# Loading keys, values and the output weights over two DMA queues in a decode kernel

## The chip, the cores and the metric

The kernel runs on one core of a Trainium2 chip. The metric is the device time of one execution in microseconds (us). Every kernel below was run several times, in turn with the kernel before on the same chip. The profiled executions give a span that is some 2 us shorter than the time (136.1 us of span go with 138.0 us). In the profiles, PE is TensorE, DVE is VectorE, ACT is ScalarE and SP is SyncE; the small q (SPq) marks an instruction that issues a load. A ring is the list of loads that one engine has issued and that are not yet done; I use the word for the queue of one issuing engine. The granted clock is the share of its full clock that TensorE ran at.

## The reference

One token of a decoder layer: attention over the last 4096 cached positions of 16 key/value heads, beside a two-layer GELU block, mixed by a sigmoid gate. Cut to what matters:

```python
# D = 576, Hq = 32, Hkv = 16, Dh = 128, window W = 4096, F = 4608, all bf16
q = (x @ wq)                                   # wq: 4.7 MB
scores = q . k[last 4096] / sqrt(128)          # k: 16 heads x 1 MB
o = softmax(scores) . v[last 4096]             # v: 16 heads x 1 MB
a = o @ wo                                     # wo: 4.7 MB
b = gelu(x @ w1 + b1) @ w2 + b2                # w1, w2: 5.3 MB each
g = sigmoid(sum(x * gate_w))
return g * a + (1 - g) * b
```

Every weight and every cached key and value is used once. The work is to move 53.6 MB from HBM, the chip's main memory, into the core.

## The kernel before

All large loads are issued from SyncE, on one queue, in the order w1, wq, K, V, wo, w2. K and V tiles of 1 MB share a pool of 8 buffers. The parts that matter here:

```python
    kv_pool = ctx.enter_context(tc.tile_pool(name="kv_pool", bufs=8, side="right"))
    ...
    for h in range(Hkv):                              # scores
        k_t = kv_pool.tile([P, NCH * Dh], BF16, name="kv_t", tag="kv")
        nc.sync.dma_start(out=k_t[:], in_=A_k_cache[0, h, Sk - W : Sk, :]...)
        kt = early[:, (h % 2) * W : (h % 2 + 1) * W]
        nc.vector.transpose(out=kt.bitcast(FP32), in_=k_t[:].bitcast(FP32))
        ...                                           # 8 matmuls into s_ps
    ...                                               # softmax -> pt
    for h in range(Hkv):                              # values
        v_t = kv_pool.tile([P, NCH, Dh], BF16, name="kv_t", tag="kv")
        nc.sync.dma_start(out=v_t[:], in_=A_v_cache[0, h, Sk - W : Sk, :]...)
        for c in range(NCH):
            nc.tensor.matmul(o_ps[:, 2 * h : 2 * h + 2], lhsT=v_t[:, c, :], ...)
    ...
    for r in range(0, RO, 8):                         # wo: 4 chunks, 1152 KB each
        nc.sync.dma_start(out=wo_t[:, r : r + 8, :], in_=wo_src[:, r : r + 8, :])
    cuts = [(0, 0, 9), (0, 9, 18), (1, 0, 8), (1, 8, 13), (1, 13, 16), (1, 16, 18)]
    for b, j0, j1 in cuts:                            # w2: 6 chunks
        nc.sync.dma_start(out=w2_t[:, b * NJ + j0 : b * NJ + j1, :], in_=...)
    ...                                               # o_ps -> o_sb -> om -> ov
    for r in range(RO):                               # 32 pairs of products
        y_add(ov[:, r : r + 1], wo_t[:, r, :])
    for f in range(NF):                               # 36 pairs of products
        y_add(gt[:, f : f + 1], w2_t[:, f, :], stop=(f == NF - 1))
```

`y_add` makes one pair of matmuls with a single output row: 512 columns and 64 columns. I call it a pair. wo_t takes the space of wq_t, and w2_t that of w1_t, so both can load as soon as q and the hidden layer are computed. That is long before they are needed. The source order of the loads is not binding: the framework has a scheduler that orders the instructions of each engine itself, and it may move a load forward.

Of the kernel before, what the change touches and what calls it, by code (L numbers as in the profile page):

```python
# [9 lines left out]
BF16 = mybir.dt.bfloat16  # L10
# [6 lines left out]
def kernel(  # L17
# [15 lines left out]
    nc = tc.nc  # L33

    P = 128
    D = 576
    Hq, Hkv, Dh = 32, 16, 128
    Sk, W = 32768, 4096
    NCH = W // P
# [13 lines left out]
    kv_pool = ctx.enter_context(tc.tile_pool(name="kv_pool", bufs=8, side="right"))  # L53
# [72 lines left out]
    for t in range(2):  # L126
# [18 lines left out]
        out=junk_row[:],  # L145
# [17 lines left out]
        out=omg[:], in0=g_t[:], scalar1=-1.0, scalar2=1.0, op0=ALU.mult, op1=ALU.add  # L163
# [3 lines left out]
        out=b2g[:], in0=b2_row[:], scalar1=omg[0:1, 0:1], scalar2=None, op0=ALU.mult  # L167
# [38 lines left out]
    for j in range(NJ):  # L206
# [15 lines left out]
        out=poly[:],  # L222
# [50 lines left out]
    for b in range(4):  # L273
# [4 lines left out]
            out=diag[:, :, 0:512].rearrange("p h (j m) -> p h j m", m=P)[:, :, :, 0:2],  # L278
            in_=qj_ps[rows].rearrange("p j h t -> p h j t"),
# [3 lines left out]
    s_ps = ps_s.tile([P, NCH * 32], FP32, name="s_ps")  # L283
    for h in range(Hkv):
        k_t = kv_pool.tile([P, NCH * Dh], BF16, name="kv_t", tag="kv")
        nc.sync.dma_start(
            out=k_t[:],
            in_=A_k_cache[0, h, Sk - W : Sk, :].rearrange("(p c) d -> p (c d)", p=P),
        )
        kt = early[:, (h % 2) * W : (h % 2 + 1) * W]  # L290
        nc.vector.transpose(out=kt.bitcast(FP32), in_=k_t[:].bitcast(FP32))  # L291
        kv = kt.rearrange("p (c b k t) -> p c b k t", c=NCH, b=2, t=2)
        for j in range(4):
            for f in range(2):
                nc.tensor.matmul(  # L295
                    s_ps[:, f * 512 : (f + 1) * 512].rearrange("p (c k) -> p c k", k=32),
                    lhsT=qz[:, h, j, :],
                    rhs=kv[:, f * 16 : (f + 1) * 16, j // 2, :, j % 2],
                    start=(h == 0 and j == 0),
                    stop=(h == Hkv - 1 and j == 3),  # L300
                    skip_group_check=True,
                )


    m1 = const.tile([P, 1], FP32, name="m1")
# [6 lines left out]
    for b in range(4):  # L312
# [10 lines left out]
        out=e_t[:], in_=s_ps[:], func=ACT.Exp, bias=negm[:, 0:1], scale=SCALE, accum_out=sums[:]  # L323
# [13 lines left out]

    o_ps = ps_o.tile([P, Hq], FP32, name="o_ps")
    for h in range(Hkv):
        v_t = kv_pool.tile([P, NCH, Dh], BF16, name="kv_t", tag="kv")  # L340
        nc.sync.dma_start(
            out=v_t[:],
            in_=A_v_cache[0, h, Sk - W : Sk, :].rearrange("(p c) d -> p c d", p=P),
        )
        for c in range(NCH):
            nc.tensor.matmul(  # L346
                o_ps[:, 2 * h : 2 * h + 2],
                lhsT=v_t[:, c, :],
                rhs=pt[:, c, 2 * h : 2 * h + 2],
                start=(c == 0),  # L350
                stop=(c == NCH - 1),
            )
# [3 lines left out]
    wo_t = big.tile([P, RO, D], BF16, name="wo_t", tag="A")  # L356
    wo_src = A_wo.rearrange("(p r) n -> p r n", r=RO)
    for r in range(0, RO, 8):
        nc.sync.dma_start(out=wo_t[:, r : r + 8, :], in_=wo_src[:, r : r + 8, :])
    w2_t = big.tile([P, NF, D], BF16, name="w2_t", tag="B")  # L360
    w2_src = B_w2.rearrange("(b p j) n -> p b j n", b=2, j=NJ)
    cuts = [(0, 0, 9), (0, 9, 18), (1, 0, 8), (1, 8, 13), (1, 13, 16), (1, 16, 18)]
    for b, j0, j1 in cuts:
        nc.sync.dma_start(
            out=w2_t[:, b * NJ + j0 : b * NJ + j1, :], in_=w2_src[:, b, j0:j1, :]
# [6 lines left out]
    for a in range(4):  # L372
        nc.vector.tensor_scalar(
            out=om[:, :, a], in0=o_sb[:], scalar1=hi4[:, a : a + 1], scalar2=None, op0=ALU.mult
# [47 lines left out]
```

## Time and profile before

| | before |
|---|---|
| time, median | 138.0 us (137.85 to 138.01) |
| span | 136.1 us |
| bytes loaded | 53.8 MB |
| DMA rate, plateau | about 420 GB/s |
| last V product starts | 108.4 us |
| first wo product starts | 111.2 us |
| last y product ends | 133.1 us |

First, part 2 of the page of the kernel before: the span in 40 slices of 3.4 us, one digit per slice. PE and DMA are busy tenths, PEclk is the granted clock of TensorE in tenths, and GB/s is what the DMA engines moved.

```profile
PE   0099999352997978768774239453352459987891
...
PEclk9999999999999999999999655555555555799999
DMA  4999999999999999999999999999999999999940
GB/s 122 423 425 421 420 419 419 408 420 412 421 421 424 419 417 421 419 417 424 419 421 414 419 421 424 412 421 412 417 421 414 427 427 406 433 417 426 403 182 0
```

The DMA row is full from the second slice until the thirty-eighth, and the rate is flat. At 420 GB/s, 53.8 MB take 128 us. The kernel is bound by its loads from one end to the other. The page's list of DMA queues names their packets, bytes and share of the engines' time. Queue q1 belongs to SyncE and q10 to ScalarE:

```profile
q1 hardware_dynamic: 7490, 53.61, 95.6%
...
q10 hardware_dynamic: 8, 0.01, 0.0%
```

One queue alone keeps the engines occupied for 95.6% of the span. The chain of work that ended last (part 4 of the page), by engine and by line, says the same:

```profile
## 4 chain that ended last, share of the span: by engine, by line
DMA 77%; DVE 9%; PE 9%; issue 2%; SPq 1%; ACT 0%; DVEq 0%
DMA kv_t<-in_A_v_cache_dram 27%; DMA kv_t<-in_A_k_cache_dram 27%; DMA w_t<-in_B_w_dram 24%; DVE early L291 9%; PE s_ps L295 5%; PE y_ps L174 3%; PE o_ps L346 1%; SPq L76 1%; PE y_ps L177 0%; DVE out_row L390 0%; ACT out_row L389 0%; DVEq L291 0%
```

These are lines of PE's timeline before: start and duration in us, line, tiles and shapes, how many instructions were merged, and in brackets the idle time before them and what ended it.

```profile
80.34 5.26 PE L346 MATMUL o_ps<-pt,kv_t 128*128 128x2 bf16 x192 [2.59 <-DVE pt L335]
...
108.37 1.01 PE L346 MATMUL o_ps<-pt,kv_t 128*128 128x2 bf16 x32 [1.48 <-DMA kv_t<-in_A_v_cache_dram]
110.41 0.21 PE L377 MATMUL ov_ps<-lo32b,om 128*128 128x32 bf16 x1 [1.02 <-DVE om L373]
111.17 0.59 PE L174 MATMUL y_ps<-wo_t,ov 128*1 128x512 bf16 x1 [0.55 <-DMA wo_t<-in_A_wo_dram]
...
122.71 0.38 PE L174 MATMUL y_ps<-w_t,gt 128*1 128x512 bf16 x1 [0.63 <-DMA w_t<-in_B_w_dram]
...
132.75 0.38 PE L174 MATMUL y_ps<-w_t,gt 128*1 128x512 bf16 x1
```

The softmax lets the V products start at 80.34. V15, the last V tile, is consumed from 108.37, o is rearranged into ov, and the first wo product starts at 111.17. The 68 pairs end at 133.1, and here and there they wait for w2 (0.63 us in the fifth line). A pair takes 0.48 us while the granted clock is 0.50, and 0.245 us at 1.00. There were 12 slow pairs here. So about 12 x 0.48 + 56 x 0.245 = 19.5 us of products after V are hidden under the 24 us in which wo and w2 load (10.0 MB at 420 GB/s). The issue times on SyncE's queue show that order (start, time from first to last issue, line, tiles, count):

```profile
53.33 36.63 SPq L341 DMA_DIRECT2D kv_t<-in_A_v_cache_dram  x16
90.89 7.82 SPq L359 DMA_DIRECT2D wo_t<-in_A_wo_dram  x4
100.86 13.39 SPq L364 DMA_DIRECT2D w_t<-in_B_w_dram  x6
```

### The profile page before, as it was taken

Reading aid. Unit: us, or ns where it says so; the run is one execution under the profiler, and the core shown is the slowest. Engines: PE = TensorE matmul, PEld = TensorE weight load, DVE = VectorE, ACT = ScalarE, POOL = GpSimd, SP = SyncE. Lnnn points to the kernel's source line nnn. Section 1 sums busy time; section 2 is a strip of 40 time slices with the busy share of each in tenths; the row PEclk is TensorE's granted clock in tenths of the full one; section 3 lists DMA queues with packets and bytes.
Section 4 is the critical chain, followed back from the end, with each engine's and each line's share of the span. In section 5 each row is a group of like instructions: output and inputs, shape, how many; then the busy total and the mean of one; then the engine's idle time right before and its main releaser. Section 6 shows DMA issues by size and latency. Waiting matters only on the chain.

```text
span 136.1 us, 2522 instructions
## 1 busy us (share of the span) xinstructions
PE 90.0 (66%) x1140; PEld 54.9 (40%) x1140; DVE 53.4 (39%) x83; ACT 3.8 (3%) x8; POOL 0.7 (1%) x6
## 2 busy tenths in 40 slices
PE   0099999352997978768774239453352459987891
PEld 0089599341342323323231239452342433433340
DVE  5873002228689999989974250000000030000001
ACT  3000000000000000000000300000000000000001
POOL 2000000000000000000000000000000000000000
PEclk9999999999999999999999655555555555799999
DMA  4999999999999999999999999999999999999940
GB/s 122 423 425 421 420 419 419 408 420 412 421 421 424 419 417 421 419 417 424 419 421 414 419 421 424 412 421 412 417 421 414 427 427 406 433 417 426 403 182 0
DMA packets 7509, 53.79 MB, mean 395 GB/s; under 512 B 837, under 2 KB 841, under 8 KB 1481
## 3 DMA queue, kind: packets, MB, share of 16 engines
q1 hardware_dynamic: 7490, 53.61, 95.6%
q8 instruction: 9, 0.15, 0.4%
q14 instruction: 2, 0.02, 0.0%
q10 hardware_dynamic: 8, 0.01, 0.0%
HBM read 53.62 MB, written 0.00 MB: 394 GB/s over the span
## 4 chain that ended last, share of the span: by engine, by line
DMA 77%; DVE 9%; PE 9%; issue 2%; SPq 1%; ACT 0%; DVEq 0%
DMA kv_t<-in_A_v_cache_dram 27%; DMA kv_t<-in_A_k_cache_dram 27%; DMA w_t<-in_B_w_dram 24%; DVE early L291 9%; PE s_ps L295 5%; PE y_ps L174 3%; PE o_ps L346 1%; SPq L76 1%; PE y_ps L177 0%; DVE out_row L390 0%; ACT out_row L389 0%; DVEq L291 0%
## 5 line engine op out<-in xcount | busy, mean ns | idle before, releaser
L295 PE MATMUL s_ps<-early 128*128 128x512 bf16 x128 | 32.6, 401 | 10.5 <-DVE early L291 10.5
L291 DVE STREAM_TRANSPOSE early<-kv_t 128x2048 f32<-128x2048 f32 x16 | 36.6, 2304 | 3.6 <-DMA kv_t<-in_A_k_cache_dram 1.9
L346 PE MATMUL o_ps<-pt,kv_t 128*128 128x2 bf16 x512 | 15.4, 165 | 16.2 <-DMA kv_t<-in_A_v_cache_dram 13.7
L295 PEld LDWEIGHTS <-early 128*128 128x128 bf16 x128 | 12.8, 100 | 29.9 <-issue 16.3
L346 PEld LDWEIGHTS <-kv_t 128*128 128x128 bf16 x512 | 14.8, 105 | 17.1 <-DMA kv_t<-in_A_v_cache_dram 14.5
L370 DVE COPY o_sb<-o_ps 128x32 f32<-128x32 f32 x1 | 0.2, 191 | 29.1 <-PE o_ps L346 29.1
L174 PE MATMUL y_ps<-wo_t,ov 128*1 128x512 bf16 x32 | 10.9, 471 | 0.6 <-DMA wo_t<-in_A_wo_dram 0.6
L174 PE MATMUL y_ps<-w_t,gt 128*1 128x512 bf16 x36 | 9.2, 379 | 1.8 <-DMA w_t<-in_B_w_dram 1.8
L390 DVE CAST out_row<-y_ps 1x320 bf16<-1x320 f32 x1 | 0.5, 478 | 22.8 <-ACT out_row L389 22.8
L198 PE MATMUL h_ps<-xt,w_t 128*128 128x1 bf16 x144 | 9.3, 201 | 0.0
L198 PEld LDWEIGHTS <-w_t 128*128 128x128 bf16 x144 | 9.1, 167 | 0.2 <-issue 0.2
L177 PE MATMUL y_ps<-wo_t,ov 128*1 128x64 bf16 x32 | 7.0, 218 | 0.0
L177 PE MATMUL y_ps<-w_t,gt 128*1 128x64 bf16 x36 | 6.9, 192 | 0.0
L174 PEld LDWEIGHTS <-ov 128*1 128x1 bf16 x32 | 3.2, 100 | 6.6 <-issue 3.8
L245 PE MATMUL q_ps<-xt,wq_t 128*128 128x1 bf16 x128 | 3.9, 165 | 2.3 <-DMA wq_t<-in_A_wq_dram 2.3
L174 PEld LDWEIGHTS <-gt 128*1 128x1 bf16 x36 | 3.0, 84 | 4.8
L245 PEld LDWEIGHTS <-wq_t 128*128 128x128 bf16 x128 | 3.7, 105 | 2.4 <-DMA wq_t<-in_A_wq_dram 2.4
L216 DVE COPY hacc<-h_ps 128x36 f32<-128x36 f32 x1 | 0.2, 195 | 11.1 <-PE h_ps L207 11.1
L177 PEld LDWEIGHTS <-gt 128*1 128x1 bf16 x36 | 3.0, 84 | 2.1 <-issue 2.1
L140 DVE MEMSET early<- 128x4160 f32 x1 | 3.5, 3525 | 0.8 <-issue 0.8
L177 PEld LDWEIGHTS <-ov 128*1 128x1 bf16 x32 | 3.0, 94 | 0.2 <-issue 0.2
L187 PE MATMUL h_ps<-one_b,b_row 1*128 1x1 bf16 x36 | 2.4, 196 | 0.3 <-DMA b_row<-in_B_b_dram 0.3
(75 smaller groups left out, 31.5 us busy)
## 6 DMA issues: line engine op xcount, KB each, us to landing
kv_t<-in_A_k_cache_dram SPq DMA_DIRECT2D x16, 1024.0 KB, 18.2
kv_t<-in_A_v_cache_dram SPq DMA_DIRECT2D x16, 1024.0 KB, 17.5
w_t<-in_B_w_dram SPq DMA_DIRECT2D x5, 1152.0 KB, 9.0
wo_t<-in_A_wo_dram SPq DMA_DIRECT2D x4, 1152.0 KB, 20.5
wq_t<-in_A_wq_dram SPq DMA_DIRECT2D x4, 1024.0 KB, 13.6
w_t<-in_B_w_dram SPq DMA_DIRECT2D x2, 1296.0 KB
w_t<-in_B_w_dram SPq DMA_DIRECT2D x1, 720.0 KB, 22.0
w_t<-in_B_w_dram SPq DMA_DIRECT2D x1, 576.0 KB
```

The source lines that it names most:

```text
L76: nc.sync.dma_start(out=w1_m[:, k, :], in_=w1_src[:, k, :])
L140: nc.vector.memset(qz_flat.bitcast(FP32), 0.0)
L174: nc.tensor.matmul(y_ps[0:1, 0:N0], lhsT=vec, rhs=row[:, 0:N0], start=start, stop=stop, skip_group_check=True)
L177: nc.tensor.matmul(y_ps[0:1, N0:D], lhsT=vec, rhs=row[:, N0:D], start=start, stop=stop, skip_group_check=True)
L187: nc.tensor.matmul(h_ps[:, c : c + 1], lhsT=b1_row[0:1, f0 : (c // NJ + 1) * FH : NJ], rhs=one_b[0:1, 0:1], start=(c == 0), stop=False, sk ...
L198: nc.tensor.matmul(h_ps[:, c : c + 1], lhsT=w1_m[:, k, f0 : (c // NJ + 1) * FH : NJ], rhs=xt[:, k : k + 1], start=False, stop=False, skip_ ...
L216: nc.vector.tensor_copy(out=hacc[:], in_=h_ps[:])
L245: nc.tensor.matmul(q_ps[:, j : j + 1], lhsT=wq_m[:, k, j * Dh : (j + 1) * Dh], rhs=xt[:, k : k + 1], start=(k == 0 and j == 0), stop=False ...
L291: nc.vector.transpose(out=kt.bitcast(FP32), in_=k_t[:].bitcast(FP32))
L295: nc.tensor.matmul(s_ps[:, f * 512 : (f + 1) * 512].rearrange("p (c k) -> p c k", k=32), lhsT=qz[:, h, j, :], rhs=kv[:, f * 16 : (f + 1) * ...
L346: nc.tensor.matmul(o_ps[:, 2 * h : 2 * h + 2], lhsT=v_t[:, c, :], rhs=pt[:, c, 2 * h : 2 * h + 2], start=(c == 0), stop=(c == NCH - 1),)
L390: nc.vector.tensor_copy(out=out_row[:, 0:320], in_=y_ps[0:1, 0:320])
```

## The change

The intent: odd K and V tiles and every other wo chunk are issued from ScalarE instead of SyncE, so that the DMA engines are fed by two rings. The first eight V loads also move up in the source, ahead of the softmax, so that ScalarE issues its part of them before its exponential. In full:

```diff
--- before.py
+++ after.py
@@ -283,7 +283,7 @@
     s_ps = ps_s.tile([P, NCH * 32], FP32, name="s_ps")
     for h in range(Hkv):
         k_t = kv_pool.tile([P, NCH * Dh], BF16, name="kv_t", tag="kv")
-        nc.sync.dma_start(
+        (nc.sync if h % 2 == 0 else nc.scalar).dma_start(
             out=k_t[:],
             in_=A_k_cache[0, h, Sk - W : Sk, :].rearrange("(p c) d -> p (c d)", p=P),
         )
@@ -301,6 +301,16 @@
                     skip_group_check=True,
                 )
 
+    def load_v(h):
+        v_t = kv_pool.tile([P, NCH, Dh], BF16, name="kv_t", tag="kv")
+        (nc.sync if h % 2 == 0 else nc.scalar).dma_start(
+            out=v_t[:],
+            in_=A_v_cache[0, h, Sk - W : Sk, :].rearrange("(p c) d -> p c d", p=P),
+        )
+        return v_t
+
+    v_tiles = [load_v(h) for h in range(8)]
+
 
     m1 = const.tile([P, 1], FP32, name="m1")
     nc.vector.reduce_max(out=m1[:], in_=s_ps[:], axis=AX.X)
@@ -337,11 +347,7 @@
 
     o_ps = ps_o.tile([P, Hq], FP32, name="o_ps")
     for h in range(Hkv):
-        v_t = kv_pool.tile([P, NCH, Dh], BF16, name="kv_t", tag="kv")
-        nc.sync.dma_start(
-            out=v_t[:],
-            in_=A_v_cache[0, h, Sk - W : Sk, :].rearrange("(p c) d -> p c d", p=P),
-        )
+        v_t = v_tiles[h] if h < 8 else load_v(h)
         for c in range(NCH):
             nc.tensor.matmul(
                 o_ps[:, 2 * h : 2 * h + 2],
@@ -356,7 +362,9 @@
     wo_t = big.tile([P, RO, D], BF16, name="wo_t", tag="A")
     wo_src = A_wo.rearrange("(p r) n -> p r n", r=RO)
     for r in range(0, RO, 8):
-        nc.sync.dma_start(out=wo_t[:, r : r + 8, :], in_=wo_src[:, r : r + 8, :])
+        (nc.sync if r % 16 == 0 else nc.scalar).dma_start(
+            out=wo_t[:, r : r + 8, :], in_=wo_src[:, r : r + 8, :]
+        )
     w2_t = big.tile([P, NF, D], BF16, name="w2_t", tag="B")
     w2_src = B_w2.rearrange("(b p j) n -> p b j n", b=2, j=NJ)
     cuts = [(0, 0, 9), (0, 9, 18), (1, 0, 8), (1, 8, 13), (1, 13, 16), (1, 16, 18)]
```

## The prediction

> **What bounds the kernel now.** The loads. The page's 40 slices show all 16 DMA engines at 9 tenths or more from the second slice to the thirty-eighth and about 420 GB/s. 53.8 MB at that rate is 128 us of the 136.1 us span. The chain of waits agrees: DMA 77%. The last large w2 chunk releases PE at 128.6, PE runs to 133.2, the output takes until 136.1.
>
> This works because of the order of loads: V before wo before w2. The last V tile's matmuls start at 108.4 (PE's timeline); o is finished and the first wo product starts at 111.2; then 68 pairs of y products follow, 0.48 us a pair for the first 5.7 us (granted clock 0.50) and 0.245 us after (clock 1.00). These 19.6 us hide under the 24 us in which wo and w2 load.
>
> **What the change adds and moves.** No bytes and no PE or DVE instructions. Half of K, V and wo is issued from ScalarE.
>
> 1. Rate. The intent is more bandwidth from two rings. The engines show no gaps. The Trainium skill, "DMA: Bandwidth & Descriptors", section "Issuing engines are not separate DMA queues", says that all issuers' DMAs interleave on the same 16 engines and only issue time is saved; an issue here takes 0.33 us against 2.5 us for the megabyte it moves. I expect the plateau to stay at 415 to 430 GB/s.
>
> 2. Order. In the built instruction order of the changed kernel, the first two wo chunks come before the last K tiles, the last two between V1 and V4, and the first two w2 chunks before V8 to V15 on the SyncE queue. So 7.4 MB (17.5 us) that used to come after V now comes ahead of its second half. After V14 on that ring there is only 2.65 MB of w2, 6.3 us.
>
> 3. Late start of odd K tiles: ScalarE issues K1 only after its exponential at 23.3, and K3 to K7 around the q copies at 30. SyncE has four queued by then. Tiles land in pairs: the first transpose about 2 us later.
>
> **Costed, as estimates from these durations.** The total load still ends near 131. wo ahead of K (5.6 us) and pairing (about 2 us) move scores and softmax from 80 to about 88. The last V tile now lands 6.3 us before the loads end, with landing time near 126 instead of 108. Then: two V heads 2.0, o to ov 1.8, 68 pairs 19.6 (the same 5.7 us at half clock), output 2.9. Sum: 152 us span, plus the 1.9 us between span and time.
>
> **Prediction: 153.5 us**, range 147 to 159. Faster by over 2%: 0.03; within 2%: 0.04; slower: 0.93.
>
> **What would show each step.** Right: the second hardware queue carries about 20 MB; GB/s flat near 420 until about 128 us, then near zero; the chain of waits ends in V load, V products, then over 18 us of y products; the first wo product starts near 130; PE never waits for w2. Wrong on step 1: a plateau above 432. Wrong on step 2: wo products starting before 120, or waits for w2 between them.
>
> **What would make it wrong.** Two rings lifting the rate by several per cent; rings not shared evenly, which could bring V14 earlier; gaps in DMA where queue slots and buffers wait for one another; the clock staying low through all 68 pairs (up to 13 us more).

## The result and the profile after

The changed kernel takes 152.79 us (median of 4 runs, 152.51 to 153.61) against 137.95 us. The ratio is 1.109, with a 95% interval from 1.104 to 1.113. Ratios here are the mean time of one kernel's runs over the mean of the other's runs of the same rounds, so they are not quite the ratio of the medians.

Part 2 of the page after (slices of 3.8 us):

```profile
PE   0299996225968776872097117441104445699992
...
PEclk9999999999999999999569965555555555599999
DMA  5999999999999999999999999999999999700000
GB/s 142 424 426 419 418 418 412 421 420 416 422 422 422 416 420 421 417 422 422 418 423 415 423 423 419 422 421 415 422 413 422 420 414 416 292 1 0 4 0 0
```

The rate is the same as before. But the loads end in the thirty-fifth slice, near 130 us. Then the DMA is idle and PE works alone for five slices. The queues share the bytes, and together they occupy the engines for as many microseconds as one queue did: 86.4% of 150.6 us is 130 us, and 95.6% of 136.1 us is 130 us.

```profile
q1 hardware_dynamic: 4898, 34.48, 55.7%
q10 hardware_dynamic: 2600, 19.15, 30.7%
```

In the chain of work after, the y products (L174 and L177) have grown from 3% to 12%:

```profile
## 4 chain that ended last, share of the span: by engine, by line
DMA 76%; PE 14%; DVE 6%; issue 2%; SPq 1%; ACT 0%; DVEq 0%
DMA kv_t<-in_A_v_cache_dram 28%; DMA kv_t<-in_A_k_cache_dram 27%; DMA w_t<-in_B_w_dram 21%; PE y_ps L174 11%; DVE early L291 5%; PE y_ps L177 1%; PE o_ps L352 1%; SPq L76 1%; DVE om L381 0%; DVE out_row L398 0%; ACT out_row L397 0%; PE ov_ps L385 0%; DVE ov L389 0%; DVE o_sb L378 0%; DVEq L291 0%
```

PE's timeline after, from the softmax to the first wo product:

```profile
90.07 2.70 PE L352 MATMUL o_ps<-pt,kv_t 128*128 128x2 bf16 x96 [2.59 <-DVE pt L345]
...
126.00 1.86 PE L352 MATMUL o_ps<-pt,kv_t 128*128 128x2 bf16 x64 [1.40 <-DMA kv_t<-in_A_v_cache_dram]
128.89 0.21 PE L385 MATMUL ov_ps<-lo32b,om 128*128 128x32 bf16 x1 [1.02 <-DVE om L381]
129.38 0.58 PE L174 MATMUL y_ps<-wo_t,ov 128*1 128x512 bf16 x1 [0.28 <-DVE ov L389]
```

and its last product of 512 columns:

```profile
147.27 0.38 PE L174 MATMUL y_ps<-w_t,gt 128*1 128x512 bf16 x1
```

V15 is consumed 18 us later than before, and everything behind it shifts with it. The group of w2 products in the after page shows no idle time before any of its 36 instructions (last number):

```profile
L174 PE MATMUL y_ps<-w_t,gt 128*1 128x512 bf16 x36 | 9.0, 380 | 0.0
```

Before, this group had waited 1.8 us for w2; after, the weights had been there for a long time. SyncE's issues in the trace after show why:

```profile
47.33 0.33 SPq L365 DMA_DIRECT2D wo_t<-in_A_wo_dram  x1
...
65.95 0.33 SPq L365 DMA_DIRECT2D wo_t<-in_A_wo_dram  x1
...
80.95 8.19 SPq L372 DMA_DIRECT2D w_t<-in_B_w_dram  x2
91.09 11.43 SPq L306 DMA_DIRECT2D kv_t<-in_A_v_cache_dram  x4
112.74 5.79 SPq L372 DMA_DIRECT2D w_t<-in_B_w_dram  x4
```

Two wo chunks (one here, one on ScalarE's queue at 47.2) are issued amid K. Two more come amid the first V tiles, and the first two w2 chunks come before V8, V10, V12 and V14. In the kernel before, all of this came after V15.

### The profile page after: what moved, and what is told of

The parts are those of the page before. It is cut to its first block, busy times and chain, and to the rows that moved or that the text cites. A ratio compares the mean times of both kernels' runs of the same rounds, so it can differ in the third digit from the quotient of the medians.

```text
span 150.6 us, 2526 instructions
## 1 busy us (share of the span) xinstructions
PE 88.4 (59%) x1140; PEld 54.1 (36%) x1140; DVE 53.0 (35%) x83; ACT 3.8 (3%) x8; POOL 0.7 (0%) x6
## 3 DMA queue, kind: packets, MB, share of 16 engines
q10 hardware_dynamic: 2600, 19.15, 30.7%
## 4 chain that ended last, share of the span: by engine, by line
DMA 76%; PE 14%; DVE 6%; issue 2%; SPq 1%; ACT 0%; DVEq 0%
DMA kv_t<-in_A_v_cache_dram 28%; DMA kv_t<-in_A_k_cache_dram 27%; DMA w_t<-in_B_w_dram 21%; PE y_ps L174 11%; DVE early L291 5%; PE y_ps L177 1%; PE o_ps L352 1%; SPq L76 1%; DVE om L381 0%; DVE out_row L398 0%; ACT out_row L397 0%; PE ov_ps L385 0%; DVE ov L389 0%; DVE o_sb L378 0%; DVEq L291 0%
## 5 line engine op out<-in xcount | busy, mean ns | idle before, releaser
L295 PE MATMUL s_ps<-early 128*128 128x512 bf16 x128 | 33.6, 410 | 17.1 <-DVE early L291 17.0
L352 PE MATMUL o_ps<-pt,kv_t 128*128 128x2 bf16 x512 | 14.9, 165 | 25.5 <-DMA kv_t<-in_A_v_cache_dram 22.9
L174 PE MATMUL y_ps<-wo_t,ov 128*1 128x512 bf16 x32 | 9.4, 426 | 0.3 <-DVE ov L389 0.3
L174 PE MATMUL y_ps<-w_t,gt 128*1 128x512 bf16 x36 | 9.0, 380 | 0.0
L177 PE MATMUL y_ps<-w_t,gt 128*1 128x64 bf16 x36 | 6.9, 193 | 0.0
L177 PE MATMUL y_ps<-wo_t,ov 128*1 128x64 bf16 x32 | 6.6, 205 | 0.0
L174 PEld LDWEIGHTS <-ov 128*1 128x1 bf16 x32 | 2.9, 92 | 5.6 <-issue 2.0
L174 PEld LDWEIGHTS <-gt 128*1 128x1 bf16 x36 | 3.0, 84 | 4.8
L177 PEld LDWEIGHTS <-gt 128*1 128x1 bf16 x36 | 3.1, 85 | 0.0
L177 PEld LDWEIGHTS <-ov 128*1 128x1 bf16 x32 | 2.9, 89 | 0.0
```

What stands on the lines that cost most here:

```text
L174: nc.tensor.matmul(y_ps[0:1, 0:N0], lhsT=vec, rhs=row[:, 0:N0], start=start, stop=stop, skip_group_check=True)
L177: nc.tensor.matmul(y_ps[0:1, N0:D], lhsT=vec, rhs=row[:, N0:D], start=start, stop=stop, skip_group_check=True)
L295: nc.tensor.matmul(s_ps[:, f * 512 : (f + 1) * 512].rearrange("p (c k) -> p c k", k=32), lhsT=qz[:, h, j, :], rhs=kv[:, f * 16 : (f + 1) * ...
```

## The experiments

Eight kernels were run, all correct. Where an order had to be forced, the loads were chained by scheduling edges, which order the instructions that the scheduler emits and add no wait; so they fix the order on each ring, but do not hold one ring back for the other:

```python
    def in_order(keys):
        for first, then in zip(keys, keys[1:]):
            tc.add_manual_dep(loads[then].ins, loads[first].ins.name,
                              <NoSync edge>, reason="order of loads")
```

Theory A: the order of the loads costs the time, because bytes that V does not need now arrive before V, and the products behind V come out from under the loads. Theory B, the rival: two rings cost the time themselves, through tiles that arrive in pairs, late issue on ScalarE, or contention. Theory C, the intent: two rings raise the rate.

Times are medians. Spans and first wo products are those of the one profiled execution, which can be the fastest of its runs (w2 after V: 149.25 us) or the slowest (wo alone: 141.23, V15 moved: 146.29).

| run | rings | ahead of the last V tile, beyond before | first wo product | span | time | ratio (95%) |
|---|---|---|---|---|---|---|
| before | 1 | - | 111.2 | 136.1 | 138.0 | 1 |
| source move only | 1 | - | 111.3 | 136.2 | 137.99 | 1.000 (0.998 to 1.001) |
| both rings, old order | 2 | - | 113.5 | 137.0 | 138.66 | 1.005 (1.003 to 1.008) |
| wo alone on both | 2 | 2 wo chunks, 2.4 MB | 116.9 | 139.5 | 140.42 | 1.017 (1.015 to 1.019) |
| w2 after V, V15 moved | 2 | wo, 4.7 MB | 122.4 | 144.5 | 146.04 | 1.059 (1.057 to 1.060) |
| w2 after V | 2 | wo, 4.7 MB (w2 beside V15) | 125.9 | 147.5 | 150.02 | 1.087 (1.083 to 1.091) |
| w2 products ahead | 2 | wo and 2 w2 chunks, 7.4 MB | 129.1 | 146.0 | 148.16 | 1.075 (1.071 to 1.078) |
| changed kernel | 2 | wo and 2 w2 chunks, 7.4 MB | 129.4 | 150.6 | 152.79 | 1.109 (1.104 to 1.113) |
| new order on one ring | 1 | the same 7.4 MB | 128.3 | 150.1 | 152.02 | 1.101 (1.099 to 1.104) |
| all of w2 before V8 | 2 | wo and all w2, 10.0 MB | 135.6 | 157.0 | 159.13 | 1.154 (1.149 to 1.159) |

### Both rings, the old order

The changed kernel, with all wo and w2 loads behind V15:

```diff
+    # every wo and w2 load gets a scheduling edge from every V load
+    after_all((nc.sync if r % 16 == 0 else nc.scalar).dma_start(out=wo_t[...], ...))
+    after_all(nc.sync.dma_start(out=w2_t[...], ...))
```

> Both rings exactly as in the changed kernel (odd K, V and half of wo from ScalarE), but the order of loads of the kernel before is forced: all K, all V, then wo, then w2. Theory A (the order of loads costs the time, two rings in themselves are neutral): 137 to 140 us, DMA plateau near 420 GB/s, first wo product near 111 to 113 us, and the chain of waits ends in w2 loads again. Rival B (two rings in themselves cost it, by pairing of tiles, by ScalarE issuing late or by contention): above 145 us although the order is restored. Rival C (two rings raise the rate): below 135 us.

Measured: 138.66 us, 0.5% above the kernel before; the first wo product came at 113.5, a little later than the expected 111 to 113. PE's timeline of this run:

```profile
84.34 6.62 PE L368 MATMUL o_ps<-pt,kv_t 128*128 128x2 bf16 x243 [2.60 <-DVE pt L361]
...
111.00 1.01 PE L368 MATMUL o_ps<-pt,kv_t 128*128 128x2 bf16 x32 [2.23 <-DMA kv_t<-in_A_v_cache_dram]
...
113.52 0.58 PE L190 MATMUL y_ps<-wo_t,ov 128*1 128x512 bf16 x1 [0.28 <-DVE ov L405]
...
129.49 0.38 PE L190 MATMUL y_ps<-w_t,gt 128*1 128x512 bf16 x1 [0.44 <-DMA w_t<-in_B_w_dram]
```

With the order restored, 14.1 of the 14.8 us are gone, and the w2 products wait for w2 again (last line). Theory B keeps 0.7 us at most, and theory C gets nothing: the loads ran near 420 GB/s, as before. The 0.7 us has a visible counterpart. Softmax ends at 84.3 instead of 80.3, and the table of engines by stretch (length, busy time and count of PE, PEld, DVE, ACT, POOL, then clock, DMA share and GB/s) shows the one gap in the loads, in the stretch from 85 to 88 us:

```profile
85.00:88.00 3.00, 3.00 (x119) 3.00 (x116) 0.00 (x0) 0.00 (x0) 0.00 (x0) 0.50 0.90 344
```

The kernel before had a DMA share of 1.01 there. The loss from 85 to 91 us, against 420 GB/s, is (3 x 76 + 3 x 8) / 420 = 0.6 us. That the eight V buffers had run out while the softmax was late fits this, but I did not test it.

### The new order on one ring

The converse: no load from ScalarE, but the merged order of the changed kernel.

```diff
-    (nc.sync if h % 2 == 0 else nc.scalar).dma_start(...)     # K, V, wo
+    nc.sync.dma_start(...)
+    in_order(K0..K12, wo0, wo1, K13..K15, V0..V2, wo2, wo3, V3..V7,
+             w2_0, w2_1, V8..V15, w2_2..w2_5)
```

> The converse: every load from SyncE on one ring, in the merged order of the changed kernel (two wo chunks before K13, two between V2 and V3, two w2 chunks before V8). Theory A: 150 to 154 us, with the last V products near 126 to 127 and y products for over 17 us after all loads have ended. Rival B: near 138 us.

Measured: 152.02 us. Its GB/s row and PE's timeline:

```profile
GB/s 155 423 425 422 412 421 412 420 413 424 419 421 419 415 421 422 427 413 424 419 417 421 424 419 419 416 418 419 419 419 419 421 411 421 329 10 0 4 0 0
```

```profile
125.76 1.01 PE L367 MATMUL o_ps<-pt,kv_t 128*128 128x2 bf16 x32 [1.48 <-DMA kv_t<-in_A_v_cache_dram]
...
128.28 0.58 PE L189 MATMUL y_ps<-wo_t,ov 128*1 128x512 bf16 x1 [0.28 <-DVE ov L413]
```

One ring with the new order reproduces the loss to 0.8 us; the last V products start at 125.8, just before the expected 126 to 127. Together with the run before this settles theory A against B: the order carries the time, and the number of rings hardly matters (0.7 to 0.8 us in these two runs).

### The w2 products moved ahead

The order of loads on each queue is that of the changed kernel. PE does the 18 pairs of the first two w2 chunks where it waits for V8.

```diff
+        if h == 8:
+            for f in range(NJ):
+                y_add(gt[:, f : f + 1], w2_t[:, f, :], behind=o_mm)
...
-    for f in range(NF):
+    for f in range(NJ, NF):
```

A first build without the edge behind V7's products let the scheduler put nine of these matmuls ahead of all V products.

> The changed kernel with its order of loads on each queue unchanged, but PE does the 18 pairs of products of the first two w2 chunks between V7 and V8, where it sits idle for 6.9 us and where both chunks have landed. If the added time is the exposed chain of y products, 18 pairs at 0.245 us leave it: 4.4 us less than the changed kernel, 147.5 to 149.5 us, loads ending at the same time. If instead the late end is set by something else, 152.8 stays.

Measured: 148.16 us, 4.6 us less than the changed kernel. PE's timeline of this run, the first of the 18 pairs and the first wo product:

```profile
105.44 0.59 PE L189 MATMUL y_ps<-w_t,gt 128*1 128x512 bf16 x1
...
129.06 0.58 PE L189 MATMUL y_ps<-wo_t,ov 128*1 128x512 bf16 x1 [0.28 <-DVE ov L424]
```

The loads still end near 130 us and the first wo product comes within 0.3 us of the changed kernel's (129.38), but the last y product starts at 142.6 instead of 147.3. The exposed time at the end is therefore the chain of y products, pair by pair.

### All of w2 after V, with wo still early

```diff
-             w2_0, w2_1, V8..V15, w2_2..w2_5)
+             V8..V15, w2_0..w2_5)
```

> Two rings, wo early as in the changed kernel, but all of w2 after V15. Theory A: two w2 chunks (2.65 MB, 6.3 us at 420 GB/s) no longer stand before the last V tile, so it lands 6.3 us sooner and the whole tail with it: 152.8 - 6.3 = 146.5 us, range 145 to 148.5. PE then does the w2 products without waiting. Rival B: 152 to 153.

Measured: 150.02 us. The direction is that of theory A, but only about half of the 6.3 us came back. The timeline:

```profile
117.72 1.86 PE L367 MATMUL o_ps<-pt,kv_t 128*128 128x2 bf16 x64 [3.28 <-DMA kv_t<-in_A_v_cache_dram]
123.36 1.01 PE L367 MATMUL o_ps<-pt,kv_t 128*128 128x2 bf16 x32 [3.77 <-DMA kv_t<-in_A_v_cache_dram]
...
125.88 0.58 PE L189 MATMUL y_ps<-wo_t,ov 128*1 128x512 bf16 x1 [0.28 <-DVE ov L411]
```

V13 and V14 are done at 117.7 + 1.9, but V15 is used only from 123.4, where a tile takes 2.5 us to arrive elsewhere in this trace (a pair every 5.0). My sum had treated the two rings as one line. V15 was the last load on ScalarE's ring while SyncE's ring had already gone on to w2, so w2 took about half of the rate while V15 loaded. The packet records of this trace show it: from 117 to 121 us SyncE's ring moved 223 GB/s and ScalarE's 188, and from 100 to 115, with V tiles on both, 209 and 208.

### The same with V15 on SyncE's ring

```diff
-        (nc.sync if h % 2 == 0 else nc.scalar).dma_start(out=v_t[:], ...)
+        (nc.sync if h % 2 == 0 or h == 15 else nc.scalar).dma_start(out=v_t[:], ...)
```

> The run with w2 after V came out at 150.0 us, where 146.5 was expected. Its V15, alone on ScalarE's ring, landed 5.6 us after V14, while w2 loaded on the other ring. Here V15 is issued from SyncE, ahead of w2 on the same ring, and nothing else changes. If two busy rings share the engines evenly, V15 needs 2.5 us instead of about 5, and this run is 2.5 us faster: 147.0 to 148.2 us, with V15's products about 2.5 us after V14's. If the sharing has nothing to do with it, 150 stays.

Measured: 146.04 us, and V15's products follow V14's without a gap:

```profile
118.20 2.72 PE L367 MATMUL o_ps<-pt,kv_t 128*128 128x2 bf16 x96 [3.11 <-DMA kv_t<-in_A_v_cache_dram]
...
122.44 0.58 PE L189 MATMUL y_ps<-wo_t,ov 128*1 128x512 bf16 x1 [0.28 <-DVE ov L411]
```

The first wo product comes 3.4 us sooner (122.44 against 125.88) and the span is 3.0 us shorter; two more pairs ran at half clock here (10 against 8). The time fell by 4.0 us, to below the range that I had given. The runs of the version with V15 on ScalarE scattered from 149.3 to 150.9, which covers part of that difference. That the sharing delays V15 is shown; its size is some 2.5 to 3.5 us rather than exactly 2.5.

### Only wo on both rings

```diff
-        nc.sync.dma_start(out=wo_t[:, r : r + 8, :], in_=wo_src[:, r : r + 8, :])
+        (nc.sync if r % 16 == 0 else nc.scalar).dma_start(out=wo_t[...], in_=wo_src[...])
```

> The kernel before with only wo alternated; K and V stay on SyncE. The scheduler then lets ScalarE issue its two wo chunks near 29 us, before most of K, and keeps the rest after V. Theory A: 2.36 MB (5.6 us) go ahead of V, the last V products start near 114 instead of 108.4, the first wo product near 116.8, and 68 pairs (18.3 to 19.6 us) plus 2.9 us of output end at 138 to 139.5 us of span, so 140 to 141.5 us: only some 3 of the 5.6 us appear, because the kernel before had that much slack between the y products and the end of the loads. Rival B (ScalarE's ring itself costs time in proportion to the bytes on it, 2.4 of the 19 MB): below 139.8 us, 1/8 of the loss.

Measured: 140.42 us, 1.7% slower. PE's timeline:

```profile
114.11 1.01 PE L346 MATMUL o_ps<-pt,kv_t 128*128 128x2 bf16 x32 [1.48 <-DMA kv_t<-in_A_v_cache_dram]
...
116.90 0.59 PE L174 MATMUL y_ps<-wo_t,ov 128*1 128x512 bf16 x1 [0.55 <-DMA wo_t<-in_A_wo_dram]
```

Moving 5.6 us of bytes ahead of V delays the first wo product by 5.7 us and the end of the span by 3.4 us. The kernel before thus had 2.3 us of slack between its y products and the end of its loads; the waits for w2 between its pairs add up to the same 2.3 us. Both profiles have 12 slow pairs. The profiled run is the slowest of the four, whose spans reach down to 138.2 us at a higher mean clock (0.864 against 0.841), and the median time grew by only 2.4 us: with fewer slow pairs there is more slack. Beyond that slack, every microsecond of bytes put ahead of V counts. Even this small part of the change does harm alone: the built order puts one of ScalarE's two wo chunks ahead of each of its two q copies, behind its first exponentials. Theory B had put this run below 139.8 us.

### All of w2 before V8

```diff
-             w2_0, w2_1, V8..V15, w2_2..w2_5)
+             w2_0..w2_5, V8..V15)
```

> The changed kernel with the last four w2 chunks (2.65 MB, 6.3 us) also ahead of V8 to V15. Theory A: the last V products move from 126 to about 132 and the tail with them: 152.8 + 6.3 = 159 us, range 157.5 to 161. Rival B (rings): no change, 152 to 153.

Measured: 159.13 us. Another 6.3 us of bytes went ahead of V, and 6.3 us were added:

```profile
121.97 1.86 PE L367 MATMUL o_ps<-pt,kv_t 128*128 128x2 bf16 x64 [16.97 <-DMA kv_t<-in_A_v_cache_dram]
...
132.24 1.86 PE L367 MATMUL o_ps<-pt,kv_t 128*128 128x2 bf16 x64 [0.60 <-DMA kv_t<-in_A_v_cache_dram]
...
135.62 0.58 PE L189 MATMUL y_ps<-wo_t,ov 128*1 128x512 bf16 x1 [0.28 <-DVE ov L412]
```

PE sits idle for 17 us before V8 and then has all 68 pairs still to do.

### Only the move in the source

The diff with its first eight V loads moved up, but every load still from SyncE.

> Only the move of the first eight V loads up in the source, all on SyncE. The built order of loads is that of the kernel before, so both theories give 138 us, within 0.5%. If it is slower, the move itself costs something that the order of loads does not show.

Measured: 137.99 us, ratio 1.000. The move is harmless. Built without the move but with both queues (built, not run), the instructions of SyncE and ScalarE come out in exactly the order of the changed kernel. So what brings wo and w2 forward is the second queue. With one queue the scheduler kept the loads in source order. With two, it placed wo and w2, which were free to load early, between K and V loads that had to wait for a buffer. That it did so because of those waits is my reading and was not tested.

## Why the prediction was right

1. The bound and the rate. Right. The plateau is about 420 GB/s with one ring and with two (a mean of 419 from 3.5 to 130 us in both traces), as the Trainium skill's "DMA: Bandwidth & Descriptors", section "Issuing engines are not separate DMA queues", led me to expect. The queue of ScalarE carried 19.15 MB (expected about 20). The run with both rings and the old order isolates it: no gain, and 0.5% lost.
2. The order. Right, and shown from both sides: undoing the order alone brings 138.66 us, imposing it alone brings 152.02 us. The turn of the last two V tiles came at 126.0 (expected near 126), the first wo product at 129.4 (near 130), and PE never waited for w2. V14 on SyncE's ring was the last V tile to arrive, as expected: the last packet on ScalarE's ring started at 124.6.
3. The late K tiles. Right in direction, too small in size. I had 5.6 us for wo and about 2 us for pairing, so the V products at 88; they began at 90.07. The run with both rings and the old order gives 4.0 us for the rings alone (84.34 against 80.34). Of these, 2.3 us come at the start, and not from pairing as I had it: K1 was issued on the other ring at 23.1, beside the last wq chunk, and that chunk landed late (30.8 instead of 28.4), so q was late. That the other 1.7 us are pairing is likely, but not shown. PE's timeline after, where the last wq products had no wait before the change:

```profile
27.14 1.01 PE L245 MATMUL q_ps<-xt,wq_t 128*128 128x1 bf16 x32 [1.59 <-DMA wq_t<-in_A_wq_dram]
30.81 0.59 PE L254 MATMUL q_ps<-xl,wq_t 128*128 128x2 bf16 x16 [2.65 <-DMA wq_t<-in_A_wq_dram]
```

   None of this mattered to the sum, since V was the last to arrive anyway.
4. The tail. V to wo 3.4 us (expected 3.8), 68 pairs 18.3 us (expected 19.6), output 2.9 us (expected 2.9). The pairs were quicker because only 6 of them ran at half clock, where I had taken over the 12 of the kernel before: 6 x 0.235 = 1.4 us. The Trainium skill's "TensorE: Matmul & The Clock Gate", section "What's actually happening", says that the clock follows activity in a free-running window, so that the number of cold matmuls varies from run to run. The traces fit: 6, 7, 8, 8, 10, 10, 12, 12 and 12 slow pairs in the nine profiled kernels whose products I counted (in the run with w2 products ahead, 6 at each of its two starts). These are different kernels; for one kernel there is only the mean clock of its runs. The four runs of the changed kernel had 0.830, 0.827, 0.820 and 0.819, with spans of 150.6, 150.6, 151.8 and 151.3 us, and the profiled one is among the shorter. So the 1.4 us are in part the luck of that execution.

The sum of the result reads: the first wo product 18.2 us later, less 2.3 us of slack that the kernel before had, less 1.4 us of clock, is 14.5 us, and the span grew by 14.5 us. That the 153.5 us lies only some 0.7 us from the result owes something to luck too: the terms of the prediction add up to 152.3 us of span and so to 154.2 us, and the errors of the parts behind V (0.4 us up to wo, 1.3 us for the pairs) all lie on one side. The same sum for the run with w2 after V and V15 moved is 11.3 - 2.3 - 0.5 = 8.5 us, and its span grew by 8.4 us.

No tested version beats the kernel before. It already moves its bytes at the plateau from 3 to 130 us, and at that rate no order of the same bytes ends the loads sooner.

## What to carry to other kernels

With the DMA engines already full on one queue, a second queue added no bandwidth here, but it lost an order of loads that the scheduler had kept on the single queue: read the built order of loads before you trust a change of queue. In a kernel bound by its loads, the bytes with the longest work behind them should arrive first; here each microsecond of bytes moved ahead of V cost one microsecond at the end, once 2.3 us of slack were used up. When the last tile of a series is alone on one ring while the other ring has gone on to the next tensor, it can take about twice as long (here 5.6 us behind the pair before it, against 2.5 us a tile otherwise), so the tile that everything waits for belongs on the ring of that next tensor, ahead of it.

## What the Trainium skill lacked or had wrong

- "DMA: Bandwidth & Descriptors", table of specifications: it gives about 358 GB/s as the HBM limit per core, half of what a stack gives to two cores. Read alone, the row is too low for this kernel, which runs on one core: the traces here hold about 420 GB/s for over 120 us (the same table's fabric ceiling of 435 GB/s is not exceeded). It is a gap of the table and no error of the page, which further down calls its higher measured rates those of a single core.
- The same page, section "Issuing engines are not separate DMA queues": it says that the engines' loads interleave and that only issue time is saved. The page gives no time for what this can cost a kernel that waits for one tile: V15, alone on one ring beside w2 on the other, came 5.6 us after the pair before it instead of 2.5 us, and moving it to the other ring took 3.0 us off the span.
- No page says that a second queue lets a scheduler bring later loads forward. Here that moved 7.4 MB ahead of V and cost 14.8 us.
- "TensorE: Matmul & The Clock Gate", section "What's actually happening": it speaks of about 3.4 us of cold work and advises against fitting a count. The dense y products here ran at half rate for 2.9 us (6 pairs) to 5.8 us (12 pairs), which is up to 1.4 us between kernels whose y products are the same (6 x 0.235 us). In the kernel before, the loads hid it.
